# An adaLN block with sliding attention and an MLP: eighteen attention blocks, transposes by DMA, modulations in column groups

## The chip, the cores and the metric

The kernel runs on one core of a Trainium2 chip. The metric is device time in microseconds (us). The engines are PE (TensorE, matmuls; PEld is its weight load), DVE (VectorE), ACT (ScalarE), POOL (GpSimd) and SP (SyncE, which here only issues DMAs). Each engine works through its own queue in order; semaphores make them wait for one another.

## The reference

One sequence of S = 2048 tokens, width D = 448, 16 heads of 28, MLP width F = 1792, all bf16.

```python
mod = (_silu(c) @ w_mod).reshape(1, 6, 1, -1)
sa, ca, ga, sb, cb, gb = mod[:, 0], ..., mod[:, 5]
h = _layernorm(x) * (1 + ca) + sa
x = x + ga * attention(h, wqkv, wo)      # each token sees 8 keys: itself and 7 back, 2 apart
h = _layernorm(x) * (1 + cb) + sb
x = x + gb * mlp(h)                      # layernorm again, w1 + b1, tanh-gelu, w2 + b2
```

Because the keys lie 2 apart, even and odd tokens never meet. The kernel treats them as two sequences of 1024 tokens in which a token sees itself and 7 direct predecessors.

## The kernel before

**Plan and order.** The body describes about 700 pieces of work ("ops") to a class `Plan`: for each its engine or engines with a cost, what it needs, which buffers it takes. `Plan.order` lists them greedily by estimated start and by the length of the work that depends on them, corrected by hand-set tables (`PRI`, `NUDGE`, `LOOK`, and `LANDS` with assumed landing times of loads). The instructions are then written out in that order, so the order on every engine is fixed at build time; a late instruction holds all behind it on its engine.

**Front end.** x is loaded in pieces into `x_all`. Per 128-token block: statistics (`stats`, L446), reciprocal deviation on POOL (`rstd`, L469, L471), normalised block `zbuf` (L477 on ACT or L480 on DVE), transposed by PE (L577, blocks 0 to 7) or by DMA on SP's queue (L569, blocks 8 to 15), then scaled and shifted into `hT` with the columns of ca and sa (`mod1`, made from 32 one-column matmuls, L511). `Wqk` is copied from a staging tile with each head padded from 28 to 32 rows (L434, L436); q and k are projected by L599 into PSUM and cast to `qT`, `kT`. Filler matmuls on a zero tile (`idle`, L379) stand between the first ops on PE.

**Attention.** 17 blocks of 121 queries (`BQ`) against 128 keys (`BK`). Per block g: scores `lt` (L678: 16 matmuls of 28 rows over four row groups), four exponentials `ex` (L689, ACT), mask `mk` (L696, DVE, times a full 128 x 16 x 128 tile `mask_rest`), values `pv` (L711) and their copy into `vbuf`, product `po` (L721) whose last column is the sum, its reciprocal (L728), the division into `on` (L732), then `pt`: four PE transposes (L742) into PSUM and `ot`, a copy into `oT` (L434 on DVE or L436 on ACT). `hT`, `qT` and `kT` have 16 columns of padding at each end.

**Output projection and MLP.** Per 128-token block b: `wo` (L763), `x1` (L768: PSUM plus x into `x_all`), second layernorm in pairs of blocks (statistics, `rstd`, z, times 1 + cb, plus sb at L787), third statistics, `ybuf`, transposed by DMA on SP (L803) into `yT`. The MLP runs in four chunks of 512 tokens: w1 (`mains`, L295, and `ends`, L300, 64-row halves), gelu on ACT (L812), w2 (L853), the bias and residual (`fin`, L866 and L868; for the blocks in `XPE` the bias gb * b2 is added by an extra matmul, L851, and DVE has one addition less), and the output DMA on SP (L872). `PHASES` says how many attention blocks come before each chunk.

**Later modulations.** ga, sb, cb and gb are made by `mod_item`: `silu_bc`, silu(c) repeated over 128 columns, against `wmod2` (L623), which gives a row repeated on all partitions in PSUM. ga scales `wo_s` (L631), gb scales `w2_s` (L648) and b2.

**Queues.** All loads after the first few go out on SP's queue in written order, then the transposes and outputs in the plan's order. Each DMA issue also waits for the DMA eight places earlier in the kernel to have landed, since they share eight semaphores in turn.

Of the kernel before, what the change touches and what calls it, by code (L numbers as in the profile page):

```python
# [17 lines left out]
KOFF_N = [0, 128, 256, 320]  # L18
ZR_N = 64
# [3 lines left out]
PADF = 16  # L23
BQ, BK = 121, 128
NBK = -(-S // BQ)
WT = PADF + S + PADF
# [5 lines left out]
PHASES = [9, 14, 17, 17]  # L32
# [4 lines left out]
LANDS = [("c", 3.0), ("x0", 5.1), ("wmsa", 6.2), ("wmca", 6.8), ("x2", 8.3), ("wk", 8.6), ("wq", 10.2), ("later", 10.0),  # L37
         ("wv", 11.4), ("x4", 12.4), ("wmod2", 17.4), ("wo", 19.1), ("b2", 19.1), ("x8", 22.0), ("w1", 28.7),
         ("w2", 31.0)]

NIDLE = [8, 3, 3, 4]
PLANS = None

LOOK = 0.000444

PRI = {"ad": -96.0, "agfst": 196.2, "ags2": 257.8, "ags3": 51.1, "ex": -118.3, "ge": -9.0, "h": 492.2,
       "lt": 26.7, "mk": -63.3, "ml": 15.5, "mod": -71.9, "on": -63.1, "ot": -130.2, "pb": -18.2, "po": 77.9,
       "ps": 105.4, "pt": 35.7, "pv": 19.9, "qe": -91.5, "qk": -123.7, "r3": 22.0, "rd": -24.1, "s2": -207.6,
       "s3": 72.9, "ve": -158.2, "w1": -18.3, "w2": -62.8, "wo": -144.0, "wt": 10.8, "x1": 20.5, "y": -37.1,
       "yt": -87.3, "z": 139.3, "z2": 81.0, "zt": -267.4}  # L50

NUDGE = {"ad10": -20.7, "ad6": -81.4, "ad8": 11.5, "ags2_0": 10.6, "ags2_11": -6.6, "ags2_14": -75.9,
       "ags2_2": -100.4, "ags2_5": -6.3, "ags2_8": -10.9, "ags3_11": -15.8, "ags3_14": 104.5, "ags3_3": 36.6,
       "ags3_5": -16.0, "ags3_7": -64.8, "ex11.2": 12.3, "fin9": -40.2, "frs12a": 19.8, "frs8a": 22.6,
       "ge2.10": 13.7, "ge2.8": 76.9, "ge3.12": 31.1, "h12.0": 37.1, "h4.2": 55.2, "h8.2": 78.5, "lt0": 93.2,
       "lt10": 29.5, "lt12": 5.8, "lt13": 52.0, "lt15": -33.2, "lt2": -20.6, "lt4": 58.9, "lt8": -8.9,
       "mk5": 34.4, "mk8": 47.0, "ml10": -42.6, "ml4": 10.8, "on12": -18.4, "on4": 8.5, "ot11": 74.0,
       "ot12": 9.8, "ot16": 53.8, "ot4": 60.9, "ot5": 22.7, "ot6": 65.9, "out13": -24.4, "out14": -59.4,
       "out8": -106.6, "pb_cbe": -184.9, "pb_gb": -36.7, "pb_gbe": -13.6, "po0": 8.9, "po1": -60.3, "po12": 10.8,
       "po15": -157.0, "pt10": 41.4, "pt12": 14.3, "pt5": -52.4, "pt8": -37.2, "pv1": -38.0, "pv13": -62.4,  # L60
       "pv4": 11.4, "pv7": 25.6, "qe12.0": -27.8, "qe12.3": 18.7, "qe12.5": 61.8, "qe2.0": -34.0, "qe2.1": 132.4,
       "qe2.2": 4.0, "qe2.3": 19.6, "qe2.4": 7.9, "qe2.6": 9.4, "qe2.7": -33.6, "qe4.0": 62.7, "qe4.7": -12.7,
       "qe8.0": 5.1, "qe8.1": -64.2, "qe8.7": -80.1, "qk0.1": 133.8, "qk12.0": 113.6, "qk12.6": 61.1,
       "qk4.1": -47.9, "qk4.3": 67.4, "qk4.4": 55.2, "qk4.5": -100.0, "qk4.7": 76.7, "qk8.7": -37.3,
       "r2_0": -89.0, "r2_0a": 57.1, "r2_10": 15.5, "r2_4": -9.3, "r2_6": -40.7, "r2_8": -62.2, "r3_0": 23.2,
       "r3_0a": 24.8, "r3_10a": -7.1, "r3_12": -88.9, "r3_12a": -80.6, "r3_6": 21.3, "r3_6a": -73.9, "r3_8": 9.0,
       "r3_8a": 38.0, "rd12": 24.6, "rd13": 26.1, "rd4": 14.1, "rd6": 54.8, "s2_11": 64.8, "s2_15": -82.0,
       "s2_5": -15.7, "s2_6": 35.8, "s2_8": 10.9, "s3_0": -51.5, "s3_1": 12.8, "s3_10": 26.8, "s3_11": 17.0,
       "s3_12": 28.7, "s3_13": -42.2, "s3_7": 38.2, "s3_9": -24.9, "w1_0.5": 32.1, "w1_1.6": 54.9, "w1_2.0": 6.1,
       "w1_2.2": -19.8, "w1_3.6": 57.3, "w2_11.1": 53.2, "w2_14.2": 103.0, "w2_14.3": 80.6, "w2_14.6": -16.7,  # L70
       "w2_15.2": -35.7, "w2_4.3": -44.4, "w2_5.6": 48.3, "w2_8.2": 135.9, "w2_9.2": 147.8, "w2_9.3": -21.2,
       "w2_9.4": -70.7, "w2_9.5": 107.8, "w2s2": 74.7, "wo0": 8.8, "wo1": 19.3, "wo11": -16.1, "wo8": 34.2,
       "wt_0.5": -16.3, "wt_2.3": -8.1, "wt_2.5": 20.1, "x1_1": 21.7, "x1_10": -25.3, "x1_11": -5.0,
       "x1_5": 27.9, "y11": -18.1, "y5": 40.1, "yt1": 28.5, "yt10": -133.2, "yt11": -10.4, "yt12": -68.4,
       "yt2": 6.1, "z1": 95.3, "z2": 138.5, "z2_10": 23.2, "z2_11": -10.3, "z2_12": -125.8, "z2_13": 16.8,
       "z2_2": 8.2, "z2_4": 21.3, "z2_5": 19.0, "z2_8": 41.6, "z2_9": 13.3, "z4": 6.2, "z8": 12.9, "zt13": -4.0,
       "zt4": 5.5, "zt8": 84.8}
STATS_ACT = 2.0
Z_DMA = (2, 3)

XPE = (0, 1, 2, 3, 15)
# [158 lines left out]
def kernel(  # L240
# [68 lines left out]
    hT = cst.tile([128, KT, WT], BF16, name="hT")  # L309
    qT = cst.tile([128, 4, WT], BF16, name="qT")  # L310
    kT = cst.tile([128, 4, WT], BF16, name="kT")
# [5 lines left out]
    silu_bc = cst.tile([128, KT, 128], BF16, name="silu_bc")  # L317
# [9 lines left out]
    g2_bc = cst.tile([128, D], BF16, name="g2_bc")  # L327
    sb_bc = cst.tile([128, D], BF16, name="sb_bc")
    gb_bc = cst.tile([128, D], BF16, name="gb_bc")
    gbb2_bc = cst.tile([128, D], FP32, name="gbb2_bc")  # L330
    ident = cst.tile([128, 128], BF16, name="ident")
    mask1 = cst.tile([128, BK], BF16, name="mask1")
    mask_rest = cst.tile([128, H, BK], BF16, name="mask_rest")
# [4 lines left out]
    ybufs = [cst.tile([128, DP], BF16, name=f"ybuf{i}") for i in range(NYB)]  # L338
    NVB = 3
    vbufs = [cst.tile([128, H, DH + 1], BF16, name=f"vbuf{i}") for i in range(NVB)]  # L340

    wmod2 = cst.tile([128, KT, 4 * D], BF16, name="wmod2")
# [3 lines left out]
    silu_bf = cst.tile([128, KT], BF16, name="silu_bf")  # L346
# [8 lines left out]
    nc.sync.dma_start(out=c_row[:], in_=c)  # L355
    wmod = stp.tile([128, KT, 2, DP], BF16, name="wmod")
    wqk_st = stp.tile([128, KT, 2 * D], BF16, name="wqk_st")
    nc.scalar.dma_start(out=x_all[:, 0:2, :], in_=xv[:, 0, 0:2, :])
    load_ktiles(nc.sync, wmod[:, :, 0, 0:D], w_mod[:, 0:D], 0)
    load_ktiles(nc.scalar, wmod[:, :, 1, 0:D], w_mod[:, D:2 * D], 0)  # L360
    nc.scalar.dma_start(out=x_all[:, 2:4, :], in_=xv[:, 0, 2:4, :])
    load_ktiles(nc.sync, wqk_st[:, :, D:2 * D], A_wqkv[:, D:2 * D], 0)
    load_ktiles(nc.sync, wqk_st[:, :, 0:D], A_wqkv[:, 0:D], 0)
    load_ktiles(nc.sync, Wv, A_wqkv[:, 2 * D:3 * D], 0)
    nc.sync.dma_start(out=x_all[:, 4:8, :], in_=xv[:, 0, 4:8, :])
    load_ktiles(nc.sync, wmod2, w_mod[:, 2 * D:6 * D], 0)
    load_ktiles(nc.sync, wo_s, A_wo, ZR_N)
# [14 lines left out]
    c_col = stp.tile([128, KT], FP32, name="c_col")  # L382
    nc.vector.memset(c_col[:], 0.0)
    nc.vector.memset(wmod[64:128, KT - 1, :, :], 0.0)
    nc.vector.memset(wmod[:, :, :, D:DP], 0.0)
# [4 lines left out]
    nc.vector.memset(wo_s[0:ZR_N, KT - 1, :], 0.0)  # L390
# [9 lines left out]
    pad_ranges = [(0, PADF), (PADF + S, WT)]  # L400
    for (a, b) in pad_ranges:
        nc.gpsimd.memset(hT[:, :, a:b], 0.0)
        nc.gpsimd.memset(kT[:, :, a:b], 0.0)
        nc.gpsimd.memset(qT[:, :, a:b], 0.0)
    nc.gpsimd.memset(mask1[:], 1.0)
    nc.gpsimd.affine_select(out=mask1[:], in_=mask1[:], pattern=[[1, BK]], compare_op=ALU.is_ge,
                            fill=0.0, base=WIN - 1, channel_multiplier=-1)
    nc.gpsimd.affine_select(out=mask1[:], in_=mask1[:], pattern=[[-1, BK]], compare_op=ALU.is_ge,
                            fill=0.0, base=0, channel_multiplier=1)

    def tok_col(b):
        return PADF + b * 128

    def kr_of(kt):
        return 128 if kt < KT - 1 else 64

    e_c = stp.tile([128, KT], FP32, name="e_c")
    ca1_col = cst.tile([128, KT], FP32, name="ca1_col")
    sa_col = cst.tile([128, KT], FP32, name="sa_col")
    nc.gpsimd.memset(share[:], 1.0 / 64)  # L420
    nc.gpsimd.memset(wmod2[64:128, KT - 1, :], 0.0)
    for vb in vbufs:
        nc.gpsimd.memset(vb[:, :, DH:DH + 1], 1.0)
# [8 lines left out]
    def copy(e, out, in_):  # L432
        if e == "DVE":
            nc.vector.tensor_copy(out=out, in_=in_)  # L434
        else:
            nc.scalar.copy(out=out, in_=in_)  # L436

    def stats(nm, tile_key, n, i, src, **kw):

        def fn(e):  # L440
# [3 lines left out]
            if e == "DVE":  # L444
                st = T["st", nm] = sm.tile([128, 6], FP32, name="st", tag="st")
                nc.vector.bn_stats(out=st[:], in_=src())  # L446
            else:
                nm_ = sm.tile([128, 1], FP32, name="nm", tag="nm")
                nc.scalar.activation(out=junk[:], in_=src(), func=ACT.Identity, scale=-1.0 / D, accum_out=nm_[:])
                nc.scalar.activation(out=junk[:], in_=src(), func=ACT.Square, bias=nm_[:], accum_out=mv[:, i, 1:2])  # L450
                nc.scalar.mul(out=mv[:, i, 0:1], in_=nm_[:], mul=-1.0)
                nc.scalar.mul(out=mv[:, i, 1:2], in_=mv[:, i, 1:2], mul=1.0 / D)
# [53 lines left out]
    def col_fn(v):  # L506
        if v == 0:
            T["ps_col"] = ps_of("ps_col", 2 * KT)
# [426 lines left out]
```

## Time and profile before

| | |
|---|---|
| median of three runs | 182.43 us (182.28 to 182.54) |
| the profiled execution | 182.19 us, of which its span 180.48 us |
| granted TensorE clock | 1.0 |
| PE idle before an instruction | L379 1.4, L599 0.9 (for ACT Wqk), L295 0.5 us (for DMA yT) |
| first projection matmul, first MLP matmul, last matmul ends | 10.32, 66.48, 177.3 us |
| DMA transposes | 24, 2.5 us each from issue to landing (median) |
| load of w2, the last | issued 16.71, 13.7 us to landing |

The span begins with the first instruction and ends with the last; what the host's side adds lies outside. In the tables of engine time, each number is the busy time of an engine within a stretch with the count of its instructions. The chain of waits follows back from the last instruction what released what. A group's line gives busy time and mean of one instruction, then the engine's idle time just before them and what ended it.

### The profile page before, as it was taken

What the parts mean: (1) busy time and instruction counts of PE and PEld (TensorE: products, weight loads), DVE (VectorE), ACT (ScalarE), POOL (GpSimd) and SP (SyncE); (2) the same over time, 40 slices, a digit from 0 to 9 for tenths busy, and PEclk for the clock granted to TensorE, in tenths of its full rate; (3) what the DMA queues carried; (4) which work ended last, traced back from release to release, by engine and by line L of the source; (5) the groups of instructions that cost most, each with busy time, mean ns of one, the idle gap of its engine ahead of it and who ended that gap; (6) DMA issues with size and microseconds to landing.
All of it is one profiled execution on the core that took longest, in us unless ns stands there. A gap on an engine that the chain in (4) does not pass through costs nothing.

```text
span 180.5 us, 3837 instructions
## 1 busy us (share of the span) xinstructions
PE 174.4 (97%) x1464; PEld 88.4 (49%) x1464; DVE 138.4 (77%) x348; ACT 118.6 (66%) x217; POOL 32.7 (18%) x67
## 2 busy tenths in 40 slices
PE   6989999999999999999999999999999999999992
PEld 2457566555555544444655454445643454433451
DVE  5789899799998999997989988688879865020251
ACT  2298996999898946999578475995835810077400
POOL 8413005000106403121403041100013400000000
PEclk9999999999999999999999999999999999999999
DMA  5999995441000530011051012031000025100011
GB/s 166 322 368 315 401 390 162 94 86 29 0 4 0 61 61 0 0 35 32 22 79 35 4 21 63 0 73 41 0 4 25 0 56 120 47 25 0 0 51 51
DMA packets 23376, 14.63 MB, mean 81 GB/s; under 512 B 13693, under 2 KB 22398, under 8 KB 23358
## 3 DMA queue, kind: packets, MB, share of 16 engines
q1 hardware_dynamic: 22334, 13.53, 27.0%
q10 hardware_dynamic: 1024, 0.86, 1.5%
q8 instruction: 11, 0.18, 0.4%
q14 instruction: 7, 0.06, 0.1%
HBM read 9.41 MB, written 1.84 MB: 62 GB/s over the span
## 4 chain that ended last, share of the span: by engine, by line
PE 72%; DVE 12%; DMA 4%; ACT 4%; SPq 2%; issue 2%; ACTq 1%; POOL 1%; DVEq 0%
PE ps L295 21%; PE ps L853 20%; PE ps L599 8%; PE ps L763 6%; PE ps L711 5%; PE ps L300 4%; DVE st L446 4%; DMA hT<-zbuf 3%; PE ps L721 3%; PE ps L678 2%; DVE et L696 2%; PE ps L742 2%; SPq L803 2%; DVE hT L589 2%; DMA yT<-ybuf 1%
## 5 line engine op out<-in xcount | busy, mean ns | idle before, releaser
L812 ACT ACTIVATE hm<-ps,b_col 128x512 bf16<-128x512 f32 x56 | 34.1, 692 | 23.2 <-PE ps L300 23.1
L853 PE MATMUL ps<-w_s,hm 128*128 128x448 bf16 x224 | 47.2, 353 | 0.0
L469 POOL TENSOR_TENSOR rs<-tv,neg_half 128x2 f32<-128x2 f32 (+1 forms) x21 | 20.4, 973 | 108.8 <-DVE ng L465 108.7
L295 PE MATMUL ps<-yT,w_s 128*128 128x512 bf16 x168 | 39.5, 380 | 0.5 <-DMA yT<-ybuf 0.5
L689 ACT ACTIVATE et<-ps 128x512 bf16<-128x512 f32 x68 | 36.1, 613 | 3.3 <-PE ps L678 3.0
L599 PE MATMUL ps<-hT,Wqk 128*128 128x512 bf16 (+1 forms) x160 | 31.3, 337 | 0.9 <-ACT Wqk L436 0.9
L853 PEld LDWEIGHTS <-hm 128*128 128x128 bf16 x224 | 21.0, 98 | 19.3 <-issue 0.9
L295 PEld LDWEIGHTS <-w_s 128*128 128x128 bf16 x168 | 15.5, 98 | 21.9 <-issue 5.3
L866 DVE TENSOR_TENSOR xt<-ps,gbb_bc 128x448 f32<-128x448 f32 x11 | 6.9, 624 | 22.3 <-PE ps L853 22.3
L696 DVE TENSOR_TENSOR et<-et,mask_rest 128x2048 bf16<-128x2048 bf16 x17 | 20.5, 1208 | 0.1
L599 PEld LDWEIGHTS <-Wqk 128*128 128x128 bf16 x160 | 14.6, 97 | 11.4 <-POOL nb L471 1.1
L446 DVE BATCH_NORM_STATS2 st<-x_all 128x6 f32<-128x448 bf16 x32 | 18.5, 613 | 0.1
L711 PE MATMUL ps<-Wv,hT 128*128 128x448 bf16 x68 | 15.7, 353 | 0.0
L763 PE MATMUL ps<-wo_s,oT 128*128 128x448 bf16 x64 | 14.1, 352 | 0.0
L768 DVE TENSOR_TENSOR x_all<-ps,x_all 128x448 bf16<-128x448 f32 x16 | 9.7, 619 | 3.1 <-PE ps L763 3.0
L436 ACT CAST vbuf<-ps 128x448 bf16<-128x448 f32 x14 | 7.6, 546 | 5.0 <-PE ps L711 5.0
L436 ACT CAST qT<-ps 128x512 bf16<-128x512 f32 (+1 forms) x19 | 9.6, 518 | 2.0 <-PE ps L599 1.5
L721 PEld LDWEIGHTS <-et 128*128 128x128 bf16 x272 | 9.0, 96 | 3.8 <-DVE et L696 0.9
L732 DVE TENSOR_TENSOR on<-ps,rden 128x448 bf16<-128x448 f32 x17 | 10.5, 616 | 0.2
L436 ACT CAST kT<-ps 128x512 bf16<-128x512 f32 (+1 forms) x18 | 8.9, 512 | 1.3 <-PE ps L599 1.1
L721 PE MATMUL ps<-vbuf,et 128*128 128x29 bf16 x272 | 9.5, 176 | 0.1
L446 DVE BATCH_NORM_STATS2 st<-z 128x6 f32<-128x448 bf16 x16 | 9.4, 612 | 0.1
(98 smaller groups left out, 188.7 us busy)
## 6 DMA issues: line engine op xcount, KB each, us to landing
w_s<-in_B_w_dram SPq DMA_DIRECT2D x2, 896.0 KB, 11.4
out_dram<-x_all SPq DMA_DIRECT2D x16, 112.0 KB, 1.7
w_s<-in_B_w_dram SPq DMA_DIRECT2D x1, 1568.0 KB, 13.7
wmod<-in_w_mod_dram SPq DMA_DIRECT2D x1, 1344.0 KB, 7.5
x_all<-in_A_x_dram SPq DMA_DIRECT2D x1, 896.0 KB, 10.4
wqk_st<-in_A_wqkv_dram SPq DMA_DIRECT2D x2, 336.0 KB, 5.8
x_all<-in_A_x_dram ACTq DMA_DIRECT2D x2, 224.0 KB, 4.2
x_all<-in_A_x_dram SPq DMA_DIRECT2D x1, 448.0 KB, 5.0
```

The lines of the kernel that those rows point to most:

```text
L295: nc.tensor.matmul(o, lhsT=lhs(w, slice(0, 128), kt), rhs=rhs(slice(0, 128), kt), start=(i == 0), stop=False)
L436: nc.scalar.copy(out=out, in_=in_)
L446: nc.vector.bn_stats(out=st[:], in_=src())
L469: nc.gpsimd.tensor_tensor(out=rs[:], in0=T["tv", tile_key][:], in1=neg_half[:, 0:n], op=ALU.pow)
L599: nc.tensor.matmul(pq, lhsT=Wqk[:, kt, m, :], rhs=hT[:, kt, c0:c0 + w], start=(kt == 0), stop=(kt == KT - 1))
L689: nc.scalar.activation(out=et_v[:, r], in_=T["lt", g][r].rearrange("p (ft c) -> p ft c", ft=4), func=ACT.Exp, scale=float(DH) ** -0.5)
L696: nc.vector.tensor_tensor(out=et[:], in0=et[:], in1=mask_rest[:], op=ALU.mult)
L711: nc.tensor.matmul(pv, lhsT=hT[:, kt, k0:k0 + BK], rhs=Wv[:, kt, :], start=(kt == 0), stop=(kt == KT - 1))
L721: nc.tensor.matmul(po[:, h, :], lhsT=T["et", g][:, h, :], rhs=vbufs[g % NVB][:, h, :], start=True, stop=True)
L763: nc.tensor.matmul(pw, lhsT=oT[:, kt, jb * 128:(jb + 1) * 128], rhs=wo_s[:, kt, :], start=(kt == 0), stop=(kt == KT - 1))
L812: nc.scalar.activation(out=T["hm", c][:, ft, 0:w], in_=ps_of(f"p1_{c}.{ft}", w), func=ACT.Gelu_apprx_tanh, bias=b1_col[:, ft:ft + 1])
L853: nc.tensor.matmul(T["p2", b], lhsT=T["hm", c][:, ft, bi * 128:(bi + 1) * 128], rhs=w2_s[:, ft, :], start=(ft == 0 and b not in XPE), stop ...
```

## The change

All orders are made anew from new tables (`LANDS`, `PRI`, `NUDGE`, `LOOK`, `PHASES`, `NIDLE`), and these parts differ:

- **Blocks.** 18 instead of 17: in each of the two sequences one block of 128 queries and eight of 112, so that no block crosses from one sequence to the other and no padding is needed. Masks are two 128 x 128 tiles, repeated over the heads by the access pattern; the first 16 columns of each row of `et` beyond a 112 block are filled with ones once.
- **Output transposed by DMA.** `pt` and its copy go; `ot` is one DMA transpose from `on` into `oT`, issued by SP.
- **Later modulations as column tiles.** `silu_bc` is 32 columns wide on 112 partitions; 16 matmuls put the four vectors into four column groups of one PSUM tile; one copy adds 1 to the cb row; four rows go to DRAM and come back repeated on all partitions as `mod_bc`, both DMAs on ACT's queue. `wo_s`, `w2_s`, b2 and z are scaled from there.
- **x1.** `tensor_tensor_reduce` adds and sums the row into `x1_sum`; where the plan puts the second statistics on ACT (five blocks), they are three ACT operations that start from that sum.
- **Loads and fills.** c goes on ACT's queue, x0 first on SP, then w_mod's first two parts as one DMA on 112 partitions, k and q weights, then x of blocks 2 and 3. POOL's fills of masks, `et`, `on`, `vbuf` come after the first `rstd`.
- **Smaller.** Wqk is copied in eight pieces; the front end's PE transposes use four PSUM banks instead of two; `XPE` is block 15 alone; fillers are 12, 2 and 2 deep as `NIDLE` says, with those between the two column products gone.

```diff
-PHASES = [9, 14, 17, 17]
+BLOCKS = [(p * SL + t, n) for p in range(2) for t, n in [(0, BK)] + [(BK + 112 * i, 112) for i in range(8)]]
+PHASES = [9, 16, 18, 18]
-NIDLE = [8, 3, 3, 4]
+NIDLE = [12, 3, 2, 2]
-XPE = (0, 1, 2, 3, 15)
+XPE = (15,)
...
-    nc.sync.dma_start(out=c_row[:], in_=c)
+    nc.scalar.dma_start(out=c_row[:], in_=c)
...
-    nc.scalar.dma_start(out=x_all[:, 0:2, :], in_=xv[:, 0, 0:2, :])
-    load_ktiles(nc.sync, wmod[:, :, 0, 0:D], w_mod[:, 0:D], 0)
-    load_ktiles(nc.scalar, wmod[:, :, 1, 0:D], w_mod[:, D:2 * D], 0)
-    nc.scalar.dma_start(out=x_all[:, 2:4, :], in_=xv[:, 0, 2:4, :])
+    nc.sync.dma_start(out=x_all[:, 0:2, :], in_=xv[:, 0, 0:2, :])
+    nc.sync.dma_start(out=wmod[:, :, 0:2 * D], in_=w_mod[:, 0:2 * D].rearrange("(kt p) n -> p kt n", p=KM))
     load_ktiles(nc.sync, wqk_st[:, :, D:2 * D], A_wqkv[:, D:2 * D], 0)
     load_ktiles(nc.sync, wqk_st[:, :, 0:D], A_wqkv[:, 0:D], 0)
+    nc.sync.dma_start(out=x_all[:, 2:4, :], in_=xv[:, 0, 2:4, :])
...
-                nc.scalar.activation(out=junk[:], in_=src(), func=ACT.Identity, scale=-1.0 / D, accum_out=nm_[:])
-                nc.scalar.activation(out=junk[:], in_=src(), func=ACT.Square, bias=nm_[:], accum_out=mv[:, i, 1:2])
-                nc.scalar.mul(out=mv[:, i, 0:1], in_=nm_[:], mul=-1.0)
-                nc.scalar.mul(out=mv[:, i, 1:2], in_=mv[:, i, 1:2], mul=1.0 / D)
+                nc.scalar.mul(out=nm_[:], in_=total, mul=-float(D) ** -1.5)
+                nc.scalar.activation(out=junk[:], in_=src(), func=ACT.Square, scale=float(D) ** -0.5, bias=nm_[:],
+                                     accum_out=mv[:, i, 1:2])
+                nc.scalar.mul(out=mv[:, i, 0:1], in_=total, mul=1.0 / D)
...
+    def pb_fn(e):
+        pb = T["pb"] = ps_of("pb", D)
+        for kt in range(KT):
+            for v in range(4):
+                nc.tensor.matmul(pb[32 * v:32 * v + 32, :], lhsT=silu_bc[:, kt, :], rhs=wmod2[:, kt, v * D:(v + 1) * D],
+                                 start=(kt == 0), stop=(kt == KT - 1), tile_position=(0, 32 * v))
...
+    P.add("modw", {"ACT": 0.45}, needs=["pb_e"], lag=2.0,
+          fn=lambda e: nc.scalar.dma_start(out=mod_dram[:], in_=mod_rows[0:128:32, :]))
+    P.add("modr", {"ACT": 0.45}, needs=["modw"], lag=3.0,
+          fn=lambda e: nc.scalar.dma_start(out=mod_bc[:], in_=mod_dram[:].partition_broadcast(128)))
...
-            nc.vector.tensor_tensor(out=et[:], in0=et[:], in1=mask_rest[:], op=ALU.mult)
+            et = ets[g % NET][:, :, 0:nq]
+            nc.vector.tensor_tensor(out=et, in0=et, in1=masks[nq < BK][:, 0:nq].unsqueeze(1).to_broadcast([128, H, nq]),
+                                    op=ALU.mult)
...
-                nc.tensor.transpose(out=pt[:, kt, :], in_=T["on", g][:, KOFF_N[kt]:KOFF_N[kt] + 128],
-                                    identity=ident[:])
...
+        P.add(f"ot{g}", {"SP": 1.25}, needs=[f"on{g}"] + old, uses=[f"on{g}"], lag=1.2,
+              fn=lambda e: nc.sync.dma_start_transpose(out=oT[:, :, c0:c0 + nq], in_=on_of[g][0:nq, :]))
...
-              fn=lambda e: nc.vector.tensor_tensor(out=x1_blk(b), in0=T["pw", b], in1=x_all[:, b, :], op=ALU.add))
+              fn=lambda e: nc.vector.tensor_tensor_reduce(out=x1_blk(b), in0=T["pw", b], in1=x_all[:, b, :], scale=1.0,
+                                                          scalar=0.0, op0=ALU.add, op1=ALU.add,
+                                                          accum_out=x1_sum[:, b:b + 1]))
```

## The prediction

> **What bounds the kernel now.** First the slices and busy shares of the page, then the table of engine time by stretches (us, busy us and instructions of each engine).
>
> ```profile
> span 180.5 us, 3837 instructions
> PE 174.4 (97%) x1464; PEld 88.4 (49%) x1464; DVE 138.4 (77%) x348; ACT 118.6 (66%) x217; POOL 32.7 (18%) x67
> ...
> DVE  5789899799998999997989988688879865020251
> ...
> 30.00:46.00 16.00, 15.87 (x196) 8.48 (x194) 14.67 (x36) 14.07 (x29) 0.43 (x3) 1.00 0.34 67
> 46.00:66.00 20.00, 19.98 (x208) 10.75 (x205) 19.14 (x48) 17.29 (x34) 5.81 (x8) 1.00 0.19 28
> ```
>
> PE is occupied all along, but the page warns that this is not PE at its peak, so I took the price of each PE group from the chain of waits, where pieces are not overlapped (start, us, what):
>
> ```profile
> 11.76 0.81 PE ps L599 x6
> ...
> 22.79 2.12 DVE st L446 x4
> ...
> 30.82 3.15 DMA hT<-zbuf
> ...
> 59.16 0.22 PE ps L742 x4
> ...
> 60.43 0.34 PE ps L678 x16
> ...
> 62.82 0.39 PE ps L721 x16
> ...
> 64.74 0.76 PE ps L711 x4
> ...
> 65.72 0.76 PE ps L623 x4
> 66.48 2.72 PE ps L295 x12
> ...
> 95.77 0.20 PE ps L851
> ```
>
> Until 45.75 us the chain is mostly DVE (statistics, masks) and its transposes; from there to 146.5 it is PE without a gap. Multiplying every matmul group of the kernel by such rates gives 164.8 us of PE work. The first full projection runs at 11.7 us (its Wqk arrives by 11.76), the last matmul ends at 177.3: 165.6 us, so PE has only about 1.4 us of slack in all. The first MLP matmul (L295, 66.48) divides the run: 54.3 us of PE work before it, 110.4 after it in 110.8 us. At that point two paths meet: the fourth transpose of y was issued about 63.8 and with the 2.5 us of its DMA row landed near 66.3, just as PE came free. So DVE, 47.5 of 50.3 us busy between 12 and 62.3, limits this point as much as PE does.
>
> **PE, part by part.** Removed: 17 output transposes (L742); 14 of them take 3.41 us in the chain, 0.244 each, so 4.1. The four modulation products (L623) take 4 x 0.76 = 3.0. Four rows of bias (L851, XPE from five blocks to one) 4 x 0.20 = 0.8. Added: an eighteenth block, 0.34 (L678) + 0.39 (L721) + 0.76 (L711) = 1.5. The score matmuls of 16 blocks shrink from 128 to 112 columns: at most an eighth of 0.34, 0.04 x 16 = 0.6; at least nothing; I take 0.4. The modulations return as 16 matmuls in four column groups. No row shows column groups; the bounds are one after another, 16 x 0.19 = 3.0, and four at a time, 0.8. The nearest row is L678, whose 16 matmuls over four row groups take 0.34, while 16 streams of 128 columns at L711's rate (0.19 us for 448) would take 0.87; groups do overlap, so I take 0.8. Sum: -4.1 - 3.0 - 0.8 + 1.5 - 0.4 + 0.8 = -6.0. By the place in the new order, 3.2 of it falls before the first MLP matmul (54.3 to 51.1) and 2.8 after it.
>
> The Trainium skill (TensorEngine Tiling (Array Packing), Key Properties) says that different tiles can run their matmuls in parallel and that changing the tiling mode drains the engine; by it the sum keeps 0.8, against 3.0 if the row L623's rate held for each; a drain has no row of its own here.
>
> **DVE, up to the last y of the first chunk.** Prices by the rows:
>
> ```profile
> L696 DVE TENSOR_TENSOR et<-et,mask_rest 128x2048 bf16<-128x2048 bf16 x17 | 20.5, 1208 | 0.1
> ...
> L768 DVE TENSOR_TENSOR x_all<-ps,x_all 128x448 bf16<-128x448 f32 x16 | 9.7, 619 | 3.1 <-PE ps L763 3.0
> ...
> L434 DVE COPY oT<-ps 128x484 bf16<-128x484 bf16 x9 | 3.7, 407 | 0.2
> ...
> L648 DVE TENSOR_TENSOR w_s<-w_s,gb_bc 128x1792 bf16<-128x1792 bf16 x1 | 1.1, 1083 | 0.0
> ```
>
> Removed there: four copies of oT 1.6; mask_rest's fill 0.69; g_bc 0.61; the wo_s scaling from PSUM, 2.01, becomes one from SBUF, 1.08 by L648's 1792 row, which also shows that a broadcast operand keeps this rate; masks, 8 x 1.21 become 7 x 1.08 + 1.21, -0.9; two statistics go to ACT, 2 x (0.61 + 0.17) = 1.6; two zbuf 0.8, one vbuf 0.6, small ones 0.4. In all -8.1. Added: four copies of Wqk at 0.27, 1.1; five casts of 512 columns of q and k at 0.69 and two of 256 at 0.42, 4.3; four x1 with a sum. The sum's price has no row: at least nothing over 0.619, at most a second pass like the statistics' 0.613; I take 0.1, a small accumulator read, nearest to the aggregate's 0.17. So 0.4. Net -2.3. ACT in that stretch (45.1 of 50.3) loses oT copies and four or five casts and gains two sums of squares of about 0.76 + 2 x 0.2: less work than before.
>
> **The start.** x0 goes first and its statistics can run about 1.3 us earlier, but h needs mod1. The 12 fillers behind c: eight took 3.35 us from 3.50, three later ones 0.81, so 12 end at 7.9; then 32 column matmuls at 0.54 per 16 end at 9.0, and mod1 at 9.25 (9.70 before). Behind it on DVE stand three Wqk pieces (0.27) and two h (0.41): the first projection runs from 10.9 instead of 11.7, a gain of 0.8.
>
> **What gives it back.** The order is fixed, so a late instruction holds what stands behind it.
> - h of blocks 2 and 3: on ACT it stands behind eight casts (the last at 14.9), a zbuf 0.76, two vbuf 0.55 and two exponentials 1.07. It ends at 18.8; PE, which stands at this projection with all attention behind it, is there at 17.1: 1.7 lost.
> - Mask of block 2, on DVE behind eight statistics, two `on` and zbufs: about 34.3, against PE at its po 33.1: 1.2.
> - h of block 8: the fourth hT transpose cannot be issued before w2 has landed (issued 16.71, 13.7 us: 30.4) and shares SP with oT's, 1.22 us each; its DVE work stands between two masks and two x1. About 42.9 against PE at 41.5: 1.4.
>
> Together 4.3, where the kernel before lost 1.0 in this stretch. First MLP matmul: 10.9 + 50.5 + 4.3 = 65.7; the last y, 2.3 us of DVE work earlier but with about 2 us more idling, lands at the same time. I take 65.8, 0.7 earlier than now. The modulations go through DRAM: product done about 25.6, copy on ACT 0.53, an issue of about 0.45, 1.7 (an output) to 4.2 us (an early x load) to land, the same again for the way back: 30.4 to 35.4. DVE reaches wo_s at 34.3, so its work hides this but for up to 1 us, which wo0 and all behind it on PE would wait. The way back is issued on ACT and waits there for the way out; about 2.8 us of casts and exponentials lie between, so ACT stands still for at most 1.4, with a zbuf and four kT casts behind it that the second half of the q and k products needs. I put nothing on top of the waits above for it.
>
> Hidden with room: x of blocks 2 and 3, now loaded behind Wk and Wq, is needed by DVE at 11.8 and earlier landed 4.2 us after its issue; the fills moved behind the first POOL power (16 of 0.2 to 0.3, about 3.3 us from 7.6) end at 10.9, before the second power is wanted at 13.5; if either were late, h of blocks 2 and 3 is.
>
> After that point PE bounds: 110.8 - 2.8 = 108.0, last matmul 173.8; tail 3.2 as now, span 177.0. The profiled execution took 182.19 with its span of 180.48, 1.7 outside; so 178.7, and the median shown, 182.43, is 0.24 above it: **178.9 us**.
>
> The output's new path is longer: 2.5 us of DMA against a transpose of 0.24 and a copy of 0.41 to 0.57. Its cover is the PE work between on and wo; where that is gone, 1.7 per chunk. The Trainium skill (VectorE: DVE Perf Modes, Rules for kernel authors) advises TensorE for a 128x128 transpose where PSUM will do, the DMA crossbar otherwise, which speaks against this edit; the trace agrees on latency (2.5 against under 1) but shows PE as the scarce thing. By that rule the edit loses where the cover is short, which is rival 3.
>
> **Rivals.**
> 1. The waits above don't come; only work counts: 182.43 - 6.0 - 0.8 = 175.6. For it: hT, masks and casts were nearly gapless before. Against: DVE's load falls less than PE's.
> 2. Column groups run one after another: 178.9 + 2.2 = 181.1.
> 3. Slower: the last chunk's y comes too late. From the end of block 15's wo to the first MLP matmul of the last chunk PE has 19.9 us of other work now and still waits 0.45 (153.41); in the new order 14.3. By rows the new chain is two x1 1.4, statistics 1.7, POOL 0.95, z, multiply and add 1.9, statistics 1.7, a final sum pair 1.25, y 0.4, two issues and a landing 4.7: 14.0, just covered. If it takes the 20.2 us it took before (133.2 to 153.4, with outputs ahead of it on SP), PE waits 5.9: 184.8. It decides from a chain of about 17.8. A second pass in the sum (0.61 x 4 before the first chunk, more here) works the same way and would come to about 183.5.
> 4. The edits don't take effect: excluded by the instruction order, which has no L742 group left and 18 more transposes on SP.
>
> **Chances.** Forecast 0.45, rival 1 0.24, rival 2 0.08, rival 3 0.21, others 0.02. A run can tell 0.2% from no change, here 182.07 to 182.79. Faster 0.75, same 0.04, slower 0.21. The range runs from just below rival 1 to rival 3's lower part, 175.2 to 184.0; my case alone 177 to 181.
>
> **What would show it.** In the new profile: no oT copies, PE work about 6 less; the 16 modulation matmuls in about 0.8; first MLP matmul at 65 to 66; PE waits of 1 to 2 us before the second projection and near 34 and 42; x1 at 0.62 to 0.75; transposes still 2.5. Wrong if x1 takes over 1 us, if PE waits for y before the last chunk by more than 1 us, or if the first MLP matmul starts before 63.

## The result and the profile after

The changed kernel took 180.74 us (median of 20 runs, 179.99 to 184.56) against 182.31 us for the kernel before (20 runs, 181.72 to 184.02): 0.9923 of its time, interval 0.9898 to 0.9947. It is faster, by 0.8%, where 1.9% was forecast (178.9 us). One thing is needed to read the numbers: in five of the twenty executions of the changed kernel the granted TensorE clock had a mean below 1.00 (0.991 in the profiled one, 182.77 us), and these lie 1.5 to 4 us above the median of the other fifteen, 180.5; the experiments come back to it.

The page of the changed kernel, its busy shares and slices:

```profile
span 181.1 us, 3835 instructions
...
PE 171.4 (95%) x1426; PEld 84.8 (47%) x1426; DVE 134.8 (74%) x353; ACT 114.3 (63%) x224; POOL 29.1 (16%) x69
...
PE   6998999399999999899999999999999999999992
...
PEclk9999999879999999999999999999999999999999
```

A slice is 4.5 us. PE's row has a hole in the eighth (31.7 to 36.2 us), and the clock falls in that one and the next; the kernel before had neither. The chain of waits names the cause (start, us, what):

```profile
24.40 0.90 PE ps L620 x16
...
25.32 0.30 ACT mod_rows L627
...
25.98 7.10 DMA mod_dram<-mod_rows
...
33.10 0.37 ACTq L642
...
34.24 0.57 ACT kT L413
...
34.86 1.60 PE ps L597 x4
```

The 16 modulation matmuls take 0.90 us. Then the four rows, 3.5 KB, go out to DRAM, and this takes 7.1 us to land. The way back (L642) is issued by ACT and may not be issued earlier, so ACT stands at it, and the kT casts behind it come late. The waits of ACT, DVE and PE (in total, times, longest) say the same from the other side:

```profile
ACT zbuf L454 <- DMA mod_dram<-mod_rows: 4.5, 1, 4.5
...
DVE et L690 <- ACT et L683: 3.7, 1, 3.7
...
PE ps L597 <- ACT kT L413: 3.1, 1, 3.1
```

One DMA holds ACT for 4.5 us, ACT holds DVE's mask for 3.7 and PE's projections for 3.1. The prices of the new operations, on the other hand, are those forecast. Groups with the shapes kept apart (busy us, mean ns of one):

```profile
L740 DVE CUSTOM_DVE_ANT_0 x_all<-ps,x_all 128x448 bf16<-128x448 f32 x16 | 9.7, 609 | 1.6 <-PE ps L735 1.3
...
L740 DVE DVE_READ_ACCUMULATOR2_ANT x_sum<- 128x1 f32 x16 | 1.3, 83 | 0.0
...
L643 DVE TENSOR_TENSOR wo_s<-wo_s,mod_bc 128x1792 bf16<-128x1792 bf16 x1 | 1.1, 1092 | 0.9 <-DMA mod_bc<-mod_dram 0.9
```

x1 with its sum is 0.61 plus a read of 0.08 us, and the scaling of wo_s 1.09.

The other profiles of this study let the run be cut where it matters, at the load of the gelu table ahead of the first chunk's gelu:

| profiled execution | first MLP matmul | gelu table load | from there to the end of the span | span |
|---|---|---|---|---|
| before | 66.4 | 70.8 | 109.7 | 180.5 |
| changed, first profile | 69.2 | 74.4 | 106.7 | 181.1 |
| changed, second profile | 67.7 | 72.4 | 106.7 | 179.1 |
| changed, w2 loaded late | 65.1 | 70.3 | 106.7 | 176.9 |

The last stretch is 3.0 us shorter in all three. What differs between these executions lies ahead of it: the changed kernel reaches the first gelu 1.6 to 3.6 us later than the kernel before.

### The profile page after: what moved, and what is told of

It reads as the page before. It is cut to its first block, busy times and chain, and to the rows that moved or that the text cites. A ratio compares the mean times of both kernels' runs of the same rounds, so it can differ in the third digit from the quotient of the medians.

```text
span 181.1 us, 3835 instructions
## 1 busy us (share of the span) xinstructions
PE 171.4 (95%) x1426; PEld 84.8 (47%) x1426; DVE 134.8 (74%) x353; ACT 114.3 (63%) x224; POOL 29.1 (16%) x69
## 4 chain that ended last, share of the span: by engine, by line
PE 70%; ACT 13%; DVE 9%; DMA 4%; issue 2%; ACTq 0%; DVEq 0%
PE ps L827 20%; PE ps L281 15%; PE ps L597 11%; PE ps L735 5%; PE ps L697 4%; ACT hm L786 4%; DMA mod_dram<-mod_rows 4%; PE ps L373 4%; ACT et L683 3%; PE ps L286 3%; PE ps L708 3%; DVE et L690 2%; PE ps L674 2%; DVE w_s L648 1%; DVE on L718 1%
## 5 line engine op out<-in xcount | busy, mean ns | idle before, releaser
L683 ACT ACTIVATE et<-ps 128x448 bf16<-128x448 f32 (+1 forms) x72 | 34.9, 566 | 3.8 <-PE ps L674 3.7
L446 POOL TENSOR_TENSOR rs<-tv,neg_half 128x2 f32<-128x2 f32 (+1 forms) x21 | 17.8, 845 | 112.7 <-DVE ng L442 112.7
L597 PE MATMUL ps<-hT,Wqk 128*128 128x512 bf16 (+1 forms) x160 | 30.1, 340 | 3.4 <-ACT kT L413 3.1
L840 DVE TENSOR_TENSOR xt<-ps,gbb_bc 128x448 f32<-128x448 f32 x15 | 9.3, 618 | 23.4 <-PE ps L827 23.3
L690 DVE TENSOR_TENSOR et<-et,mask 128x1792 bf16<-128x1792 bf16 (+1 forms) x18 | 19.6, 1095 | 5.1 <-ACT et L683 5.1
L697 PE MATMUL ps<-Wv,hT 128*128 128x448 bf16 x72 | 16.9, 363 | 0.0
L423 DVE BATCH_NORM_STATS2 st<-x_all 128x6 f32<-128x448 bf16 x27 | 15.9, 612 | 0.1
L740 DVE CUSTOM_DVE_ANT_0 x_all<-ps,x_all 128x448 bf16<-128x448 f32 x16 | 9.7, 609 | 1.6 <-PE ps L735 1.3
L718 DVE TENSOR_TENSOR on<-ps,rden 128x448 bf16<-128x448 f32 x18 | 10.7, 611 | 0.1
L761 DVE TENSOR_TENSOR z<-z,mod_bc 128x896 bf16<-128x896 bf16 x16 | 9.9, 617 | 0.4 <-ACT z L454 0.2
L842 DVE TENSOR_TENSOR x_all<-xt,x_all 128x448 bf16<-128x448 f32 x15 | 9.4, 625 | 0.5
## 6 DMA issues: line engine op xcount, KB each, us to landing
w_s<-in_B_w_dram SPq DMA_DIRECT2D x1, 1568.0 KB, 13.7
```

Of the source, the lines that this page charges most:

```text
L446: nc.gpsimd.tensor_tensor(out=rs[:], in0=T["tv", tile_key][:], in1=neg_half[:, 0:n], op=ALU.pow)
L597: nc.tensor.matmul(pq, lhsT=Wqk[:, kt, m, :], rhs=hT[:, kt, c0:c0 + w], start=(kt == 0), stop=(kt == KT - 1))
L683: nc.scalar.activation(out=et_v[:, r], in_=T["lt", g][r][:, 0:4 * nq].rearrange("p (ft c) -> p ft c", ft=4), func=ACT.Exp, scale=float(DH) ...
L690: nc.vector.tensor_tensor(out=et, in0=et, in1=masks[nq < BK][:, 0:nq].unsqueeze(1).to_broadcast([128, H, nq]), op=ALU.mult)
L697: nc.tensor.matmul(pv, lhsT=hT[:, kt, k0:k0 + BK], rhs=Wv[:, kt, :], start=(kt == 0), stop=(kt == KT - 1))
L718: nc.vector.tensor_tensor(out=on_of[g][:, 0:D].rearrange("p (h d) -> p h d", h=H), in0=T["po", g][:, :, 0:DH], in1=T["rden", g][:].unsquee ...
```

## The experiments

Two questions were open: does the DRAM trip of the modulations explain the missing 1.8 us (180.74 against 178.9), and through which engine does it act?

**The changed kernel again.**

> The changed kernel as it is, for a second profile of it. If the granted clock was lowered only by chance in the first profile (0.86 between 33.5 and 46 us), this one can come out at 1.00 everywhere; the way out of the modulations (mod_dram) should again take about 7 us, ACT stand about 4.5 us at the issue of the way back and PE wait about 3.1 us for kT, whatever the clock. Time 180.3 to 181.3 us.

181.43 us (11 runs, 180.68 to 184.46). In the profiled execution (180.79 us) the clock was 1.00 throughout, and the trip was shorter than expected. Its chain:

```profile
25.29 4.92 DMA mod_dram<-mod_rows
...
30.23 4.83 DMA mod_bc<-mod_dram
```

4.9 us out instead of 7.1, ACT stood 2.4 and PE waited 1.0 for kT; but 1.5 more came for DVE's division, which stood behind the wo_s scaling (DVE waited 1.6 for mod_bc). So the way out varies by some 2 us from one execution to the next, and what it takes from ACT in one it takes from DVE in another.

**The way back on POOL's queue.**

```diff
-          fn=lambda e: nc.scalar.dma_start(out=mod_bc[:], in_=mod_dram[:].partition_broadcast(128)))
+          fn=lambda e: nc.gpsimd.dma_start(out=mod_bc[:], in_=mod_dram[:].partition_broadcast(128)))
```

> The way back of the modulations (modr) is issued on POOL's queue, behind the power of blocks 8 to 11 and ahead of the next one 13 us later; ACT no longer waits for the way out. Theory A (the loss is ACT standing at that issue, with a zbuf and four kT casts behind it): ACT's 4.5 us and PE's 3.1 us go, the time falls by 2 to 3 us to about 178. Rival B (the modulations themselves are late, whoever issues them): mod_bc still lands near 37, the wo_s scaling on DVE holds the masks and the division behind it and wo0 waits on PE; PE's wait moves by some us, the time falls by less than 0.7 us.

182.41 us (12 runs, 180.79 to 183.54; 1.0001 of before, 0.9974 to 1.0029). Theory A falls. B holds for the waits, but not for the time: instead of a small gain, the kernel is slower than the changed one. The way out took 4.95, the way back 5.5, mod_bc landed at 36.1, and the waits of DVE and PE were:

```profile
DVE wo_s L643 <- DMA mod_bc<-mod_dram: 4.2, 1, 4.2
...
PE ps L674 <- DVE on L718: 3.8, 1, 3.8
```

ACT is free now, and DVE stands in its place. Who issues the way back is not the question; when it lands is. What makes this kernel slower than the changed one is, as far as the runs show, the clock: its mean was 0.978 to 0.991 in eleven of the twelve (below 1.00 in five of twenty there), and the twelfth took 180.79 us. PE's wait is now one of 3.8 us, where the second profile of the changed kernel had two, of 1.0 and 1.5.

**w2 loaded late.** In the changed kernel the load of w2 is issued at 19.4 us, and 13.7 us later it lands, at 33.1: the way out, issued at 26.0 on another queue, landed in that same moment. (In the second profile it landed at 30.2, ahead of w2 at 33.0.)

```diff
-    nc.sync.dma_start(out=w2_s[:], in_=B_w2.rearrange("(ft p) n -> p ft n", p=128))
...
             o["fn"](o["ran"])
+        if o["name"] == "zt15":
+            nc.sync.dma_start(out=w2_s[:], in_=B_w2.rearrange("(ft p) n -> p ft n", p=128))
```

> Only the load of w2 (1568 KB) is moved, behind the last hT transpose (near 51 us instead of 19.4). Theory C (the 3.5 KB way out takes 7.1 us because it lands behind the bulk loads in flight): it lands in 2 to 4 us, ACT stands at most 1 us, PE's wait for kT is under 0.7 us, the time falls by 1.5 to 3 us, and w2, landing by about 60, is in time for its scaling at 71. Rival D (7 us is the latency of a write to DRAM here): the way out stays at 6 us or more and the time stays within 0.5 us.

179.05 us (5 runs, 178.65 to 179.70; 0.9823 of before, 0.9788 to 0.9858). Theory C holds. The way out was issued at 25.6 and ACT issued the way back at 28.4 without standing, so it landed in 2.8 us or less; wo_s could be scaled at 32.9 instead of 35.2 to 37.3. PE's longest waits between 10 and 80 us, in the view of waits:

```profile
PE ps L735 <- ACT hm L786: 0.5, 1, 0.5
PE ps L708 <- DVE et L690: 0.4, 1, 0.4
PE ps L674 <- DVE on L718: 0.3, 1, 0.3
```

The row of the load itself (KB, us to landing), issued now at 48.1:

```profile
w_s<-in_B_w_dram SPq DMA_DIRECT2D x1, 1568.0 KB, 8.5
```

It lands near 56.7, long before its scaling at 67. Run again beside two other kernels it took 178.97 us (5 runs, 178.38 to 179.33; 0.9816, 0.9794 to 0.9837); there the way out took 3.5 us and ACT stood 0.9:

> The run with w2 late again, for a narrower interval and beside the next one: 178.6 to 179.7 us, the granted clock at 1.00 in every run, since PE never idles for more than 0.5 us behind 18 us.

**w1 loaded late too.**

```diff
-    load_twice(nc.sync, w1_s, B_w1)
...
+        if o["name"] == "zt11":
+            load_twice(nc.sync, w1_s, B_w1)
```

> As the run before, and the two loads of w1 (896 KB each) are moved too, behind the hT transposes of blocks 8 to 11 (near 35 us instead of 11 to 20). Theory C: the way out lands in about 2 us (an output's 1.7), the way back in 2 to 4, ACT doesn't stand at all; the time falls a little more than in the run before, by 2 to 3.5 us. Against it: w1 now meets the oT and hT transposes of blocks 12 to 15, whose 2.5 us could grow to 4 or more, with h of block 12 late by as much; then it gains less than the run before. Rival D as there.

186.38 us (4 runs; 1.0219, 1.0185 to 1.0253), much worse than expected, though its trip was the shortest: 2.4 us out and 3.9 back. Its chain:

```profile
33.73 3.40 DMA hT<-zbuf
37.12 8.12 DMA oT<-on
...
45.38 1.65 PE ps L735 x4
```

An output transpose, issued behind 1792 KB of w1, took 8.1 us instead of 2.4 (the median of the eighteen), and PE waited 7.9 for it at wo, with a mean clock of 0.972 to 0.981. It looks like the same contention with another victim: a small transfer behind bulk loads that are in flight.

**The control: w2 late in the kernel before.**

> The kernel before, with nothing changed but its load of w2, moved behind its last hT transpose. Theory C (the late load helped the changed kernel because its modulations travel through DRAM): the kernel before has no such trip, so it stays within 0.5 us of 182.3, though its hT transposes could come up to 1 us earlier. Rival E (the bulk load in flight costs any kernel, by its transposes): it falls by 1.5 us or more, and then that much of the 2.4 us is not the trip's.

182.40 us (12 runs) against 182.41 for the kernel before in the same call: 0.9989, 0.9960 to 1.0018. The late load is worth nothing in this kernel, so the 2 us that it is worth in the changed kernel belong to something that is new there. That is the trip, but also the output transposes on SP's queue; the run with the wo_s scaling moved, below, bounds their part.

**A gap on PE.** In the kernel with w2 late, PE's scores of block 3 wait for a POOL fill that starts when PE's last matmul is done, once or three times:

```diff
+    def counted(*a, **k):
+        last[0] = matmul(*a, **k)
...
+        if o["name"] == "lt3":
+            f = nc.gpsimd.memset(gap[:], 0.0)
+            wait_for([f], [last[0]], "gap")
+            for _ in range(2):
+                f = nc.gpsimd.memset(gap[:], 0.0)
+            pend.append(f)
...
```

This is the form with three fills; with one, the loop runs `range(0)`.

> As the run with w2 late, but PE is kept idle ahead of the scores of block 3 (near 32 us) by a POOL fill that starts when PE's last matmul is done: about 1.5 to 2 us of idleness, nothing else changed. Theory F (idleness of PE beyond some 3 us lowers the granted clock afterwards): this one is too short, the clock stays at 1.00 and the time rises by no more than the gap, 0.5 to 2 us.

> As the run before with three such fills, some 4 us of idleness. Theory F: the granted clock falls below 1.00 in the 3 to 10 us behind the gap in most runs, and the time rises by the gap and 1 to 2 us more (183 to 185). Rival G (the lowered clock in the first profile had nothing to do with the idleness): the clock stays at 1.00 and the time rises by no more than the gap, to at most 183.

The waits of PE (L873 is the helper `counted`), in the kernel with one fill:

```profile
PE ps L873 <- POOL gap L888: 1.9, 1, 1.9
```

and in the kernel with three, where 4 us were aimed at:

```profile
PE ps L873 <- POOL gap L891: 5.6, 1, 5.6
```

The short gap cost 0.1 us, less than the 0.5 to 2 expected (179.12, 6 runs, 178.57 to 180.90): the scores of block 3 started at 33.3 instead of 32.2, the gelu table was loaded at 70.15 instead of 70.25. PE had 1 to 2 us to spare here; by this, and by the chain, which is DVE's from 58.6 us to the gelu table, DVE and not PE set when the first gelu could start. The long gap cost 5.5 us (184.51, 6 runs, 183.53 to 185.28), with a mean clock of 0.978 to 0.991 in every run. Two stretches of the table of engine time (length; busy us and count of PE, PEld, DVE, ACT, POOL; clock, DMA share, GB/s) of the kernel with the long gap:

```profile
37.00:40.00 3.00, 2.64 (x37) 1.48 (x38) 1.44 (x6) 1.43 (x4) 0.30 (x1) 0.50 0.00 0
41.00:46.00 5.00, 5.00 (x84) 3.09 (x73) 4.77 (x13) 4.97 (x13) 1.20 (x2) 1.00 0.05 12
```

and of the changed kernel's first profile:

```profile
36.00:38.00 2.00, 2.00 (x36) 1.03 (x35) 1.09 (x2) 1.72 (x5) 0.00 (x0) 0.50 0.86 141
39.00:46.00 7.00, 6.60 (x91) 3.65 (x89) 6.84 (x21) 6.97 (x18) 1.99 (x2) 1.00 0.15 35
```

Behind the gap, and behind the 3.1 us wait of the changed kernel, PE is granted half its clock for 3.4 us in all (the slices beside these rows have 0.90 and 0.89, and 0.58 and 0.71), then the whole again; the kernel with w2 late has 1.00 there. Theory F holds for the long gap. For the short one it holds in four runs of six; the other two had a mean of 0.988 and took 180.9 us. They were not profiled, so how long PE waited in them is not known.

**DVE's order.** To the run with the way back on POOL, one move: the wo_s scaling behind the division of block 2 and some statistics. The first form put it behind block 0's output product in the program, which thereby multiplied the unscaled wo_s and did not wait:

> The run with the way back on POOL, and one DVE instruction moved: the wo_s scaling stands behind the division of block 2 and the statistics of x, ahead of the mask of block 3, so that about 1.9 us of DVE work no longer waits for mod_bc. Theory H (the trip costs what DVE stands idle; ACT's stand and PE's wait only pass it on): DVE's wait of 4.2 us shrinks by about 1.9, PE's wait of 3.8 by about as much, and the time falls by 1 to 2 us against that run (182.4 to about 180.7). If what counts is when wo0 can start (mod_bc's landing), it stays at 182 or above.

180.54 us (6 runs), not comparable for that reason. The second form put it ahead of that product:

```diff
     todo = P.order()
+    todo.remove(P.index["pb_gae"])
+    todo.insert(todo.index(P.index["wo0"]), P.index["pb_gae"])
```

> The way back on POOL, and the wo_s scaling on DVE moved behind the division of block 2 and the statistics of x, and in the program ahead of block 0's output product, which so waits for it (in the run before it didn't, and multiplied by the unscaled wo_s). Theory H (the trip costs what DVE stands idle): about 1.9 us of DVE work no longer waits for mod_bc; the scores of block 3 start at once, PE waits for wo_s instead, but only as long as mod_bc is late (near 38.5 against 35 to 36, some 2 us); 180.5 to 181.3 us. If wo0's start alone decides, nothing is gained over the run with the way back on POOL: 182 or more.

181.40 us (12 runs, 179.39 to 181.98; 0.9923, 0.9888 to 0.9957), 1.0 us less than 182.41 and just above the range expected. DVE's wait for mod_bc went from 4.2 to 0.6 us, and PE waited 2.0 at wo0, as expected. (The view of waits puts this down to ACT's exponentials, which end at 37.5 us like the scaling of wo_s; with w2 late wo0 did not wait for them.) Part of the 1.0 us is the clock: compared among runs with a mean of 0.988 to 0.991, it is 181.5 (10 runs) against 182.0 (7 runs). So DVE's idleness made 0.5 to 1 us of that kernel's time; what remains of the trip's price shows as PE's wait at wo0 and in the clock behind it (the two runs at 1.00 took 179.4 and 179.6).

This profile also bounds the rival that the control left:

```profile
27.59 6.79 DMA oT<-on
...
34.48 0.64 DVE on L718
```

With w2 in flight the first output transpose took 6.8 us, and the division of block 2, which reuses its buffer, waited for it; in the two profiles with w2 late it took 5.4 and 4.3. But the scores behind that division started at 35.2 us here and at 34.9 and 34.5 there. As an estimate from these starts, the transposes made 0.2 to 0.7 of the 2 us that the late load is worth, and the trip the rest.

**The output transposes back on PE.** In the kernel with w2 late, `ot` became four PE transposes into PSUM and a copy, as in the kernel before; the planner placed them with unchanged tables, so the order differs as well.

> As the run with w2 late, but the output transposes are again on PE (18 groups of four, a copy from PSUM each on ACT or DVE); the planner places them anew with the same priorities, so the order moves and the figure is a bound, not a price. By the prediction's first step PE has 18 x 0.24 = 4.4 us more work in a kernel that PE bounds: 183 to 184.5 us against 179.05. If the transposes by DMA had bought nothing (their latency lost on PE what their work saved), it comes out at 179 to 180.

184.23 us (10 runs, 183.20 to 184.84), 5.2 above w2 late. The groups that came back:

```profile
L731 PE MATMUL ps<-ident,on 112*128 112x112 bf16 (+1 forms) x72 | 5.9, 213 | 0.4 <-DVE vbuf L411 0.3
...
L413 ACT COPY oT<-ps 128x448 bf16<-128x448 bf16 (+1 forms) x9 | 5.0, 575 | 1.9 <-PE ps L731 1.9
...
L411 DVE COPY oT<-ps 128x448 bf16<-128x448 bf16 (+1 forms) x9 | 3.4, 385 | 1.3 <-PE ps L286 1.0 <-PE ps L731 0.2
```

The bound agrees with 4.4 us of PE work; it includes 5.0 us of ACT and 3.4 us of DVE work, and an order that was not tuned for it.

**Less on DVE.** In the kernel with w2 late, two casts of q (`qe8.0`, `qe8.1`) run on ACT, and `pb_gbe` stands behind the power that the first gelu waits for.

```diff
     todo = P.order()
+    for nm in ('qe8.0', 'qe8.1'):
+        P.ops[P.index[nm]]["ran"] = "ACT"
+    todo.remove(P.index["pb_gbe"])
+    todo.insert(todo.index(P.index["x1_6"]), P.index["pb_gbe"])
```

> As w2 late, and DVE is relieved ahead of the first chunk's gelu: two casts of q of blocks 8 to 11 go to ACT (0.69 us each on DVE), and the row for the last bias (1.7 us) is made behind the power that the first gelu waits for. Theory J (up to the first MLP matmul DVE sets the time and PE has about 2 us to spare, since a gap of 1.9 us cost nothing): y of the first chunk comes 0.5 to 1.2 us earlier, the gelu 1.5 to 3, PE's wait of 0.46 there goes; 177.7 to 178.6. If PE's own work sets it, or ACT becomes late for exponentials with the two casts, the time stays within 0.3 us of 179.05 or rises.

178.32 us (5 runs, 177.68 to 178.67; 0.9775 of before, 0.9750 to 0.9800), the fastest kernel of the study: 4.1 us below the kernel before and 0.65 below w2 late in the same call. The gelu table was loaded at 68.8 instead of 70.0, but the first MLP matmul did not come earlier in the profile (65.5 against 64.9), and the two profiled executions took nearly the same (178.35 and 178.38 us), so which of the two moves brought the 0.65, and how, is open.

## Why the prediction was right and wrong

- **PE work, -6.0.** The modulations took 0.90 (0.8 taken, rival 2's 3.0 did not come). Behind the first MLP matmul 2.2 to 2.7 us went, against 2.8 forecast; from the gelu table on 3.0. For the 18 output transposes, the run with them back on PE gave 5.2 with all that hangs on them; 4.1 was the sum's largest term, so its size is bounded, not measured. The rule on 128x128 transposes weighed in the prediction (the Trainium skill, VectorE: DVE Perf Modes, Rules for kernel authors) would have chosen PE and been slower here by that run, whose order was not tuned for it.
- **DVE prices.** x1 0.69 (0.72 taken), masks 1.08 (1.08), wo_s 1.09 (1.08): right. A second pass in the sum did not exist.
- **The start.** First projection at 9.4 to 10.7 in the profiles, 10.9 forecast: a little earlier, and different from one execution to the next.
- **What gives it back, 4.3 us.** The sum came out by luck, its parts did not: without the late trip, the second projection waited about 0.5 and later places 0.3 and 0.4, not 1.7, 1.2 and 1.4: 1.3 us with the small ones. Yet the first MLP matmul was at 65.1, near the 65.8 forecast, 54.8 us after the first projection: PE was occupied for 53.4 us of them and not for the 50.5 of the summed rates. Two errors of 3 us cancelled. Where PE's 3 us arise was not traced, so of the 3.2 us forecast to fall ahead of that matmul most did not show.
- **Two slips in its sums.** 165.6 less 164.8 leaves PE 0.8 us of slack; the 1.4 is its idle time ahead of L599 and L295. And 54.3 less 3.2 is 51.1, where the sum for the first MLP matmul has 50.5 without a reason; with 51.1 the forecast would have been 179.5.
- **The modulations' trip: the step that failed.** "1.7 (an output) to 4.2 us (an early x load) to land, the same again for the way back: 30.4 to 35.4", ACT "stands still for at most 1.4" and "I put nothing on top of the waits above for it". Measured: out 4.9 to 7.1, back 4.1 to 4.8, wo_s scaled at 35.2 to 37.3, ACT standing 2.4 to 4.5. With w2 out of the way the same trip takes 2.8 to 3.5 and about 4.2, the kernel 178.97 to 179.05 us and the span 176.7 to 176.9: the forecast's 178.9 and 177.0, as closely as that only because the errors of the point above cancel. Of the two rows I took as bounds, 1.7 is of outputs, which leave when little else is in flight (at most 120 GB/s in the slices behind 72 us, up to 401 while w1 and w2 load), and 4.2 is the page's median of two x loads, which took 2.8 and 5.7. The trace of before had a nearer row, a small load issued at 10.4 us among the bulk loads, though on their own queue:

```profile
b_bc<-in_B_b_dram SPq DMA_DIRECT2D x1, 112.0 KB, 9.1
```

- **Rivals and signs.** 3 did not come: the view of waits lists none of PE behind 85 us. 1 (175.6) was not reached even with DVE relieved. The slower mechanism that did act was one that I had priced at zero; 1.8 of the 3.5 us forecast are missing. None of the three signs of being wrong appeared, but the first MLP matmul came at 67.7 to 69.2 us in the changed kernel, not at 65 to 66.
- **PE bounds after the first MLP matmul:** right; 106.7 to 106.8 us from the gelu table to the end in every variant that kept the order behind it. Ahead of it DVE limited "as much as PE does", as the prediction's first part had it; the short gap suggests that with w2 late it limited more.

## What to carry to other kernels

Bound the latency of a small DMA by the row of a small DMA that was issued while the same bulk loads were in flight, not by its size, and by the slowest such row, not by a median; before giving data a trip through DRAM, list what is in flight at that minute and whether it can be loaded later. A DMA that must wait for another DMA should not stand in the queue of a compute engine, but moving it helps only if what it brings is not awaited by another engine just as full. And where two engines meet at one point, a short gap put into one of them (here 1.9 us for 0.1) helps to tell which of them sets the time.

## What the runs showed of the hardware

- **A small write waits for bulk loads on another queue.** 3.5 KB from ACT's queue took 4.9 to 7.1 us to be reported landed while 1568 KB of SP's queue were in flight, 2.8 to 3.5 without, and 2.4 when w1 was late too; a transpose behind 1792 KB took 8.1 instead of 2.4. The Trainium skill (DMA: Bandwidth & Descriptors, Queues, rings and completion order) says that a DMA's completion count is a write that lands only after every earlier write of the same DMA engine, across its queues, and that the engines alternate between queues by packets. The trace agrees with the first in the first profile, where the way out landed in the same moment as w2, and does not decide in the second, where it landed 2.8 us ahead of w2. No run here separates the two. The packet records kept with the traces say where the time went: with w2 in flight the first of the four rows started 4.2 to 4.3 us after the issue, with w2 late 1.3 to 1.5; so most of it passed before the data moved.
- **PE's clock falls behind a gap, to one half, in stretches of 3.4 us.** In the profiles with a lowered clock it is 0.50 for 3.4 us (6.8 behind the 3.8 us wait of the kernel with the way back on POOL, 10.2 from inside the 7.9 us wait with w1 late) and 1.00 elsewhere in the working part. One stretch makes a mean of about 0.991 over 181 us, two about 0.981, and costs a busy PE half its length, 1.7 us, on top of the wait. Behind 5.6 us of idleness the mean was 0.978 to 0.991 in 6 of 6 runs, with a wait of 3.8 us in the profile 0.978 to 0.991 in 11 of 12, with one of 3.1 us lowered in that profile, with the short gap (1.9 us in the profile, which stayed at 1.00) 0.988 in 2 of 6. The spread fits: the changed kernel, whose wait varies, reached 184.6, while w2 late stayed within 178.4 to 179.7; that the wait causes it was shown only for the gap put in on purpose. The Trainium skill (TensorE: Matmul & The Clock Gate, Part 1: The HAM clock gate) says that about one idle window of 3.4 us, free-running, halves the clock. The 3.4 us, the half and the long gap agree, but the idleness need not fill the 3.4 us: 3.1 us of waiting were enough in the changed kernel's first profile, and in the profile of the run with the unscaled wo_s PE had waited 1.4 us in the 3.4 ahead of the stretch.
